# Attention with grouped heads, one core: V of the first group moved to SyncE's queue between two query loads, K of the second group asked for later

## The chip, the cores and the metric

The kernel runs on one core of a Trainium2 chip. The metric is the device time of one execution in microseconds (us). Engines are named as in the profile: PE is the matmul engine, PEld its weight loads, ACT is ScalarE, DVE VectorE, POOL GpSimd, SP SyncE. All times in a trace count from the start of its span; the span is 1.7 us shorter than the time (520.1 and 521.82 in the profiled execution).

## The reference

```python
B, Hq, Hkv, Sq, Sk, D = 16, 32, 8, 288, 512, 128        # bf16, values N(0,1) * 0.05
k = jnp.repeat(k, Hq // Hkv, axis=1)
v = jnp.repeat(v, Hq // Hkv, axis=1)
scores = jnp.einsum("bhqd,bhkd->bhqk", q, k) * D ** -0.5
p = softmax(scores, axis=-1)
return jnp.einsum("bhqk,bhkd->bhqd", p, v)
```

There are 16 x 8 = 128 groups of one K and V with 4 x 288 = 1152 query rows. A group is three blocks of work, so there are 384 blocks, counted from 0.

## The kernel before

Each block n is a set of score matmuls into PSUM (`op_s`, line L439), an exp on ACT from PSUM to SBUF (`op_exp`, L511 and L516), and, two blocks later, twelve matmuls with V (`op_pv`, L479). PSUM holds the scores of two blocks, so score block n needs exp n - 2 to be done. Queries and most K come transposed by DMA; K of groups 0 and 1 are loaded plainly and transposed on PE (`op_kt`, L404), with a copy out of PSUM on DVE (`op_kc`, L411). V is loaded, then copied by POOL into a layout with a column of ones (`op_vc`, L568).

The order at the start of each engine (cut; `...` marks cuts):

```python
first = [lambda i=i: op_q0(i) for i in range(2)]          # SyncE: queries of group 0, in two parts
first += [lambda: op_q(1), lambda: op_k(0, 2), lambda: op_v(0, None, 1, UG), lambda: op_q(2), lambda: op_q(3)]
...
@block.tensor
def _(eng):
    op_warm(WARM, BANK, ps_o[:, 1])                        # 5 matmuls of 512 columns on constants
    op_warm(1, P, ps_o[:, 1])
    op_kt(0, range(1), 0)                                  # transposes of the first K
    op_kt(0, range(1, NJ), 1)
    op_warm(1, P, ps_s[:, 1])
    for n in range(NS):
        op_s(n)
        ...
        if n == 1:
            op_kt(1, range(NJ), 1)                         # transposes of K of group 1
        if n >= LAG:
            op_pv(n - LAG)
...
@block.scalar
def _(eng):
    op_kd(eng, 0)                                          # K of group 0, 128 KB
    op_v(0, eng, 0, 1)                                     # V of group 0, 128 KB
    op_kd(eng, 1)                                          # K of group 1, 128 KB
    eng.activation(dum[:], nc.const_aps.tensor(0.0, [P, 1], FP32), ACTF.Exp)
    for n in range(NS):
        op_exp(n)
```

Of the kernel before, what the change touches and what calls it, by code (L numbers as in the profile page):

```python
# [7 lines left out]
ACTF = mybir.ActivationFunctionType  # L8
AX = mybir.AxisListType
BF16 = mybir.dt.bfloat16  # L10
FP32 = mybir.dt.float32
# [120 lines left out]
def bass_standalone__gqa_softmax__near_ridge_kernel(  # L132
# [5 lines left out]
):  # L138
    B, Hq, Sq, D = q.shape
    _, Hkv, Sk, _ = k.shape  # L140
    P = 128
    R = (Hq // Hkv) * Sq
# [45 lines left out]
    with ExitStack() as es:  # L188
# [66 lines left out]
        dum = main.enter_context(nc.sbuf_tensor("dum", [P, 1], FP32))  # L255
# [5 lines left out]
        def need(eng, waits):  # L261

            left = []
            for (s, n) in waits:
                key = (id(eng), s)
                if seen.get(key, 0) < n:
                    seen[key] = n
                    left.append((sem[s], n))
            return left

        def emit(eng, waits, fn):
            waits = need(eng, waits)
            for (s, n) in waits[:-1]:
                eng.wait_ge(s, n)
            ins = fn()
            if waits:
                ins.wait_op(waits[-1][0], waits[-1][1], "sem-ge")
            return ins
# [3 lines left out]
        def op_kd(eng, g):  # L282
            eng.dma_start(kd_sb[:, g], kd_v[:, g]).then_inc(sem["s_kd%d" % g], 16)

        def op_k(u, g0=0):
            eng = nc.sync
            sl = u % NSLOT
            if u >= NSLOT:
                for (s, n) in need(eng, [("s_s", NC * UG * (u - NSLOT + 1))]):
                    eng.wait_ge(s, n)  # L290
            eng.dma_start_transpose(
                kt_sb[:, sl, :, g0:UG].rearrange("d j g p -> d j (g p)"),
                k_v[(u * UG + g0) * P:(u + 1) * UG * P]
            ).then_inc(sem["us_k%d" % sl if u > 0 else "s_k2"], 16)

        def op_v(u, eng=None, g0=0, g1=UG):
            eng = eng or nc.sync
            sl = u % NSLOT
            if u >= NSLOT:
                for (s, n) in need(eng, [("s_vc", UG * (u - NSLOT + 1))]):  # L300
                    eng.wait_ge(s, n)
            eng.dma_start(
                vd_sb[:, sl, g0:g1], v_v[:, u * UG + g0:u * UG + g1]
            ).then_inc(sem["us_v%d" % sl if u > 0 else "s_v%d" % g0], 16)

        def op_q(g):
            eng = nc.sync
            if g >= NQ:
                for (s, n) in need(eng, [("s_s", NC * (g - NQ + 1))]):
                    eng.wait_ge(s, n)  # L310
            eng.dma_start_transpose(qt_sb[:, g % NQ], q_v[g * P:(g + 1) * P]).then_inc(sem["s_q%d" % (g % NQ)], 16)

        def op_q0(i):

            c0, c1 = ((0, TB), (TB, NT))[i]
            nc.sync.dma_start_transpose(qt_sb[:, 0, c0:c1], q_v[0:P, c0 * D:c1 * D]).then_inc(sem["s_qp%d" % i], 16)
# [82 lines left out]
        def op_kt(g, tiles, bank):  # L399

            eng = nc.tensor
            dst = ps_o[:, bank].bitcast(BF16)
            for x, j in enumerate(tiles):
                ins = emit(eng, [("s_id", 2), ("s_kd%d" % g, 16)], lambda: eng.transpose(  # L404
                    dst[:, x * P:(x + 1) * P], kd_sb[:, g, j * D:(j + 1) * D], ident[:]))
            ins.then_inc(sem["s_kp"], 1)
# [7 lines left out]
        def op_warm(n, w, dst):  # L414

            for x in range(n):
                nc.tensor.matmul(dst[:, 0:w], nc.const_aps.tensor(1.0, [P, P], BF16),
                                 nc.const_aps.tensor(1.0, [P, w], BF16), start=True, stop=True)

        def op_s(n):  # L420
            eng = nc.tensor
            g, i = n // NC, n % NC
            sl, gi = (g // UG) % NSLOT, g % UG
            waits = [have("k", g), have_q(g, i)]
            if n >= 2 + FIRST:
                waits.append(("s_e", n - 1))
            qg = qt_sb[:, g % NQ].rearrange("d t p -> d (t p)")
            todo = pieces(i)
            for x, (c, j, t, w) in enumerate(todo):
                if shared(n) and c + w == CH:  # L430
                    w -= W
                w_x = waits if x == 0 else []
                if n == 0 and x < 2:
                    w_x = [("s_k0", 1), waits[1]] if x == 0 else waits[:1]
                if n == 1 and x < 2:
                    w_x = [have_q(g, x)]
                if 2 <= n < 2 + FIRST:
                    w_x = w_x + [ready(n - 2, c // BANK)]
                ins = emit(eng, w_x, lambda: eng.matmul(  # L439
                    ps_s[:, n % 2, c:c + w], kt_sb[:, sl, j, gi, :], qg[:, t * P:t * P + w], start=True, stop=True))  # L440
                if n < FIRST and (c + w) % BANK == 0 and c + w < CH:
                    ins.then_inc(sem["s_s0"], 1)
            ins.then_inc(sem["s_s"], 1)

        def op_sy(n):

            eng = nc.tensor
            g = n // NC
            (t, j), = [(t, j) for t in range(NT) for j in range(NJ) if place(t, j) == (n % NC, CH - P)]
            emit(eng, [("s_ev", n - LAG - 1)], lambda: eng.matmul(  # L450
                ps_o[:, (n - LAG) % 2, BANK - W:BANK], kt_sb[:, (g // UG) % NSLOT, j, g % UG, :],
                qt_sb[:, g % NQ, t, P - W:P], start=True, stop=True))
# [9 lines left out]
        def op_pv(r):  # L462
            eng = nc.tensor
            g = r // NC
            sl, gi = (g // UG) % NSLOT, g % UG
            waits = [("s_vc", g + 1)]
            if 2 <= r < NS - 2:
                waits.append(("s_ev", r - 1))
            if r == NS - 2:
                waits.append(("s_e", NS - 1))  # L470


            todo = sequence(r % NC)
            for x, (t, j) in enumerate(todo):
                i, c = place(t, j)
                w_x = (waits if x == 0 else []) + [ready(g * NC + i, c // BANK)]
                if c == CH - P and shared(g * NC + i):
                    w_x.append(("s_yp", nth(g * NC + i)))
                ins = emit(eng, w_x, lambda: eng.matmul(  # L479
                    outs(r)[:, t - r % NC * TPC, :], pt(g, t, j), v_sb[:, sl, gi * NJ + j, 0:DV], start=(x == 0),  # L480
                    stop=(t not in [y[0] for y in todo[x + 1:]]), skip_group_check=True))
            ins.then_inc(sem["s_pv"], 1)
# [36 lines left out]
        def shared(n):  # L519
            return FIRST_SHARED <= n < NS - NC and (n - FIRST_SHARED) % EVERY == 0  # L520
# [102 lines left out]
                op0=ALU.is_lt, op1=ALU.add)).then_inc(sem["s_bad"], 1)  # L623


        first = [lambda i=i: op_q0(i) for i in range(2)]
        first += [lambda: op_q(1), lambda: op_k(0, 2), lambda: op_v(0, None, 1, UG), lambda: op_q(2), lambda: op_q(3)]

        sp = []
# [14 lines left out]
        @block.sync  # L644
        def _(eng):
            for fn in first:
                fn()
            for (_, fn) in sp:
                fn()
            choose(eng, "sp")  # L650

        @block.tensor
        def _(eng):
            op_warm(WARM, BANK, ps_o[:, 1])
            op_warm(1, P, ps_o[:, 1])
            op_kt(0, range(1), 0)
# [3 lines that stand above are left out]
                op_s(n)  # L660
                if shared(n):
                    op_sy(n)
                if n == 1:
                    op_kt(1, range(NJ), 1)
                if n >= LAG:
                    op_pv(n - LAG)
            op_pv(NS - 2)
            op_pv_last()
            emit(eng, [("s_ev", NS - 2), ("s_bad", 2)], lambda: eng.matmul(  # L669
                ps_o[0:1, NS % 2, 0:ALONE + 1], one_f[:], bad_sb[:, 1, :], start=True, stop=True)  # L670
            ).then_inc(sem["s_bad"], 1)
            choose(eng, "pe")

        @block.scalar
        def _(eng):
            op_kd(eng, 0)
            op_v(0, eng, 0, 1)
            op_kd(eng, 1)
            eng.activation(dum[:], nc.const_aps.tensor(0.0, [P, 1], FP32), ACTF.Exp)  # L679
            for n in range(NS):  # L680
                op_exp(n)
            op_ev_act()
            choose(eng, "act")
# [82 lines left out]
```

## Time and profile before

| | |
|---|---|
| time, median of the first 3 runs | 522.98 us (522.68 to 523.08) |
| time of the profiled execution | 521.82 us |
| span | 520.1 us |
| first exp starts | 5.27 us |
| PE waits for the last time before the end at | 9.71 us |
| last block's exp starts | 515.08 us |

The head of the page of this profile gives the span, each engine's busy time, and the share of TensorE's clock that the throttle granted, in forty slices:

```profile
span 520.1 us, 15350 instructions
...
PE 515.1 (99%) x6224; PEld 394.2 (76%) x6224; DVE 369.6 (71%) x1315; ACT 513.3 (99%) x393; POOL 79.4 (15%) x135
...
PEclk9999999999999999999999999999999999999999
```

PE and ACT are both full, and the clock row is at 9 throughout.

### The profile page before, as it was taken

The numbers are of one execution on the slowest core, as the hardware profiler recorded it, in microseconds if no ns is written. First come the engines' busy times: TensorE is split into PE (matmuls) and PEld (weight loads), VectorE is DVE, ScalarE is ACT, GpSimd is POOL, SyncE is SP. The second block draws the span as 40 slices with busy tenths as digits, with TensorE's granted clock in tenths as the row PEclk, the third lists the DMA queues.
The fourth block names the chain that finished last, engine by engine and source line by source line (L and its number), as shares of the span: only waits on it lengthen the run. The fifth ranks groups of instructions, "written<-read, shape, count | busy, mean of one in ns | idle before, by whom it ended". The sixth has DMA issues, their size and how long they took to land.

```text
span 520.1 us, 15350 instructions
## 1 busy us (share of the span) xinstructions
PE 515.1 (99%) x6224; PEld 394.2 (76%) x6224; DVE 369.6 (71%) x1315; ACT 513.3 (99%) x393; POOL 79.4 (15%) x135
## 2 busy tenths in 40 slices
PE   8999999999999999999999999999999999999997
PEld 4777777777777777777777777777777777777776
DVE  2767767777777677776776776767767767677776
ACT  7999999999999999999999999999999999999997
POOL 2111111111111111111111111111111111111110
PEclk9999999999999999999999999999999999999999
DMA  9999999999999998999999989999999999997212
GB/s 179 237 181 265 274 183 247 235 215 211 245 210 260 210 253 183 234 227 242 235 240 190 222 229 225 238 184 224 220 231 229 225 205 199 219 226 177 90 69 93
DMA packets 253110, 110.06 MB, mean 212 GB/s; under 512 B 219760, under 2 KB 236784, under 8 KB 253040
## 3 DMA queue, kind: packets, MB, share of 16 engines
q1 hardware_dynamic: 252608, 108.69, 98.2%
q8 instruction: 49, 0.80, 0.7%
q10 hardware_dynamic: 432, 0.39, 0.3%
q14 instruction: 21, 0.17, 0.1%
HBM read 17.04 MB, written 37.75 MB: 105 GB/s over the span
## 4 chain that ended last, share of the span: by engine, by line
ACT 98%; DMA 1%; issue 1%; DVE 0%; PE 0%
ACT pt_sb L516 97%; DMA qt_sb<-in_q_dram 1%; ACT pt_sb L511 1%; DVE o_sb L585 0%; DVE o_sb L595 0%; PE ps_s L479 0%; PE ps_s L439 0%; DVE rl_sb L575 0%; PE ps_o L669 0%; DVE bad_sb L621 0%; DVE flag_i L733 0%; DVE bad_sb L618 0%
## 5 line engine op out<-in xcount | busy, mean ns | idle before, releaser
L516 ACT ACTIVATE pt_sb<-ps_s 128x1536 bf16<-128x1536 f32 (+2 forms) x384 | 508.8, 1443 | 0.0
L479 PE MATMUL ps_o<-v_sb,pt_sb 128*128 128x129 bf16 x4584 | 322.5, 220 | 0.4 <-ACT pt_sb L516 0.4
L479 PEld LDWEIGHTS ps_o<-v_sb,pt_sb 128*128 128x128 bf16 x4584 | 282.7, 98 | 50.2 <-DVE o_sb L585 14.1
L439 PE MATMUL ps_s<-qt_sb,kt_sb 128*128 128x512 bf16 (+2 forms) x1536 | 309.3, 324 | 1.0 <-DMA qt_sb<-in_q_dram 1.0
L585 DVE TENSOR_TENSOR o_sb<-ps_o,rl_sb 128x384 bf16<-128x384 f32 x382 | 211.9, 555 | 9.3 <-DVE rl_sb L575 0.5
L439 PEld LDWEIGHTS ps_s<-qt_sb,kt_sb 128*128 128x128 bf16 x1536 | 123.5, 98 | 62.3 <-DMA qt_sb<-in_q_dram 1.7
L575 DVE RECIPROCAL rl_sb<-ps_o 128x3 f32<-128x3 f32 x382 | 68.2, 178 | 126.4 <-PE ps_o L479 125.0
L568 POOL COPY v_sb<-vd_sb 128x512 bf16<-128x512 bf16 x128 | 78.4, 613 | 429.7 <-PE ps_o L479 416.2
L549 DVE SCALAR_TENSOR_TENSOR u_sb<-u_sb,m_sb 128x120 f32<-128x120 f32 x126 | 35.6, 283 | 2.2
L556 DVE SCALAR_TENSOR_TENSOR pt_sb<-u_sb,e_sb 128x120 bf16<-128x120 f32 x63 | 17.8, 283 | 2.2
L549 DVE SCALAR_TENSOR_TENSOR u_sb<-m_sb 128x120 f32<-128x120 f32 x63 | 17.5, 277 | 0.0
L527 DVE TENSOR_SCALAR y_sb<-ps_o 128x120 f32<-128x120 f32 x63 | 15.9, 253 | 0.0
L540 DVE TENSOR_SCALAR m_sb<-t_sb 128x120 int32<-128x120 int32 x63 | 14.1, 223 | 2.2
L450 PE MATMUL ps_o<-qt_sb,kt_sb 128*128 128x120 bf16 x63 | 13.6, 217 | 0.0
L540 DVE TENSOR_SCALAR e_sb<-t_sb 128x120 int32<-128x120 int32 x63 | 13.6, 216 | 0.0
L533 DVE TENSOR_SCALAR t_sb<-y_sb 128x120 int32<-128x120 f32 x63 | 13.4, 213 | 0.0
L450 PEld LDWEIGHTS ps_o<-qt_sb,kt_sb 128*128 128x128 bf16 x63 | 6.2, 98 | 7.4
L411 DVE COPY kt_sb<-ps_o 128x128 bf16<-128x128 bf16 (+2 forms) x3 | 1.0, 336 | 5.4 <-PE ps_o L404 5.3
L511 ACT ACTIVATE pt_sb<-ps_s 128x512 bf16<-128x512 f32 x6 | 3.3, 617 | 1.5 <-PE ps_s L439 1.5
L679 ACT ACT_TABLE_LOAD x1 | 1.3, 1283 | 2.2 <-issue 2.2
L613 DVE TENSOR_REDUCE st_sb<-rl_sb 128x1 f32<-128x72 f32 (+1 forms) x16 | 3.5, 217 | 0.0
L611 DVE TENSOR_REDUCE st_sb<-rl_sb 128x1 f32<-128x72 f32 (+1 forms) x16 | 3.5, 216 | 0.0
(32 smaller groups left out, 13.1 us busy)
## 6 DMA issues: line engine op xcount, KB each, us to landing
out_dram<-o_sb SPq DMA_DIRECT2D x127, 288.0 KB, 3.8
vd_sb<-in_v_dram SPq DMA_DIRECT2D x31, 512.0 KB, 5.3
qt_sb<-in_q_dram SPq DMA_TRANSPOSE x129, 5.0
kt_sb<-in_k_dram SPq DMA_TRANSPOSE x32, 5.0
vd_sb<-in_v_dram SPq DMA_DIRECT2D x1, 384.0 KB, 4.3
out_dram<-o_sb SPq DMA_DIRECT2D x3, 96.0 KB, 1.6
kd_sb<-in_k_dram ACTq DMA_DIRECT2D x2, 128.0 KB, 2.9
vd_sb<-in_v_dram ACTq DMA_DIRECT2D x1, 128.0 KB, 3.2
```

Source lines behind the costliest of these rows:

```text
L439: ins = emit(eng, w_x, lambda: eng.matmul(ps_s[:, n % 2, c:c + w], kt_sb[:, sl, j, gi, :], qg[:, t * P:t * P + w], start=True, stop=True))
L450: emit(eng, [("s_ev", n - LAG - 1)], lambda: eng.matmul(ps_o[:, (n - LAG) % 2, BANK - W:BANK], kt_sb[:, (g // UG) % NSLOT, j, g % UG, :], ...
L479: ins = emit(eng, w_x, lambda: eng.matmul(outs(r)[:, t - r % NC * TPC, :], pt(g, t, j), v_sb[:, sl, gi * NJ + j, 0:DV], start=(x == 0), st ...
L516: emit(eng, waits, lambda: eng.activation(d, s, ACTF.Exp, scale=scale)).then_inc(sem["s_e"], 1)
L527: emit(eng, [("s_yb", nth(n) - NB), ("s_pv", n - LAG + 1)], lambda: eng.tensor_scalar(out=y_sb[:, b], in0=ps_o[:, (n - LAG) % 2, BANK - W: ...
L533: emit(eng, [("s_ym", 2 * (nth(n) - NB)), ("s_y", nth(n))], lambda: eng.tensor_scalar(out=t_sb[:, b], in0=y_sb[:, b], scalar1=Y_MUL, scala ...
L540: emit(eng, [("s_yp", nth(n) - NB), ("s_yb", nth(n))], lambda: eng.tensor_scalar(out=dst[:, b], in0=t_sb[:, b], scalar1=mask, scalar2=bits ...
L549: lambda: eng.scalar_tensor_tensor(out=u_sb[:, b, x], in0=src, scalar=QUARTIC[x], in1=m, op0=ALU.add, op1=ALU.mult)
L556: lambda: eng.scalar_tensor_tensor(out=pt_sb[:, n % NPT, CH - W:CH], in0=u_sb[:, b, 2], scalar=QUARTIC[3], in1=e_sb[:, b].bitcast(FP32), o ...
L568: emit(eng, waits, lambda: eng.tensor_copy(v_sb[:, sl, gi * NJ:(gi + 1) * NJ, 0:D], vd_sb[:, sl, gi].rearrange("p (j d) -> p j d", d=D))). ...
L575: emit(eng, [("s_pv", r + 1)], lambda: eng.reciprocal(rl_sb[:, TPC * r:TPC * (r + 1)].unsqueeze(2), outs(r)[:, :, D:DV])).then_inc(sem["s_ ...
L585: emit(eng, waits, lambda: eng.tensor_tensor(out=o_sb[:, g % NO, t0:t0 + TPC, :], in0=outs(r)[:, :, 0:D], in1=rl_sb[:, TPC * r:TPC * (r + ...
```

## The change

The intent: the very first query load shares the DMA engines with three loads from ACT's queue (from 3.6 to 3.8 us the trace has 70 packets of ACT's queue to 29 of SyncE's). If only the first K runs beside it, the first scores can start sooner. V of group 0 moves to SyncE's queue, behind the first part of the queries; K of group 1 is asked for once the first K has been transposed, and its transposes move behind score block 2.

```diff
-        first = [lambda i=i: op_q0(i) for i in range(2)]
+        first = [lambda: op_q0(0), lambda: op_v(0, None, 0, 1), lambda: op_q0(1)]
...
-                if n == 1:
+                if n == 2:
                     op_kt(1, range(NJ), 1)
...
             op_kd(eng, 0)
-            op_v(0, eng, 0, 1)
+            eng.activation(dum[:], nc.const_aps.tensor(0.0, [P, 1], FP32), ACTF.Exp)
+            for (s, n) in need(eng, [("s_k0", 2)]):
+                eng.wait_ge(s, n)
             op_kd(eng, 1)
-            eng.activation(dum[:], nc.const_aps.tensor(0.0, [P, 1], FP32), ACTF.Exp)
```

## The prediction

> **What bounds the kernel now.** I read the page's chain first, then asked the trace whether the engine it names really sets the pace, then went through the first 14 us, the only place the change touches.
>
> The chain that ended last names ScalarE (ACT) for nearly the whole span, with one DMA wait ahead of it:
>
> ```profile
> ACT 98%; DMA 1%; issue 1%; DVE 0%; PE 0%
> ```
>
> But section 1 of the page has PE as busy as ACT (both 99%), so I compared single exps with the score matmuls they read, in the timeline of a stretch in mid-kernel (start, duration, engine, line, operation):
>
> ```profile
> 262.76 0.82 PE L439 MATMUL ps_s<-qt_sb,kt_sb 128*128 128x512 bf16 x6
> 263.63 1.45 ACT L516 ACTIVATE pt_sb<-ps_s 128x1536 bf16<-128x1536 f32 x1
> 264.10 0.81 PE L439 MATMUL ps_s<-qt_sb,kt_sb 128*128 128x512 bf16 x3
> 264.96 1.45 ACT L516 ACTIVATE pt_sb<-ps_s 128x1536 bf16<-128x1536 f32 x1
> ```
>
> The scores end at 263.58 and 264.91 and the exps start 0.05 us later each: ACT waits for PE by a hair at every step, although the page books no idle time, because consecutive exps overlap. PE goes from one matmul to the next without a gap, one step per 1.33 us. So **PE is the bound** from some early point on, and any delay of PE after that point is final. The waits of PE give that point; there are only these:
>
> ```profile
> PE ps_o L669 <- DVE bad_sb L621: 1.0, 1, 1.0
> PE ps_s L439 <- DMA qt_sb<-in_q_dram: 1.0, 2, 0.8
> PE ps_o L417 <- PEq L751: 0.9, 1, 0.9
> PE ps_o L479 <- ACT pt_sb L516: 0.4, 1, 0.4
> ```
>
> The first is the final check, the third the start. The last one, in the timeline, is the turning point:
>
> ```profile
> 4.84 1.04 PE L439 MATMUL ps_s<-qt_sb,kt_sb 128*128 128x512 bf16 x4 [0.81 <-DMA qt_sb<-in_q_dram]
> 5.27 1.08 ACT L511 ACTIVATE pt_sb<-ps_s 128x512 bf16<-128x512 f32 x2 [1.52 <-PE ps_s L439]
> 8.09 0.81 PE L439 MATMUL ps_s<-qt_sb,kt_sb 128*128 128x512 bf16 x3
> 9.71 0.40 PE L479 MATMUL ps_o<-v_sb,pt_sb 128*128 128x129 bf16 x4 [0.36 <-ACT pt_sb L516]
> 10.85 1.17 POOL L568 COPY v_sb<-vd_sb 128x512 bf16<-128x512 bf16 x2 [5.77 <-DMA vd_sb<-in_v_dram]
> 11.93 0.84 PE L479 MATMUL ps_o<-v_sb,pt_sb 128*128 128x129 bf16 x12
> ```
>
> The first queries land at 4.79, PE starts the scores at 4.84, ACT starts exp 0 at 5.27 and runs exps 0, 1 and 2 without a gap. PE waits at 9.71 for exp 2, which ends at 9.65 (start 8.14 plus 1.51). From 9.71 PE never waits again until the final check. The end is thus 9.71 plus PE's work. What moves 9.71, or makes PE wait after it, moves the end one for one; nothing else does.
>
> [...] from 3.2 to 3.6 us both queues have packets, and then K of group 1 crowds out the transposes. [...] the first query load issues in 1.3 us and lands 4.0 us after its start. The activation-table load [...] is 1.28 us here and ends by 3.54, off the path in both kernels.
>
> **The change part by part.**
>
> (1) *ACT's queue loses V (128 KB) and has K of group 1 (128 KB) later.* Before, the packets of both run from 2.9 to 4.4 us, beside the first query load. Its own packets (512 of 256 bytes) run at about 0.1 us per 50 between 2.4 and 3.2 and end at 3.6 to 3.9, and it lands about 0.9 later. I estimate 3.4 for their end without that traffic, so a landing at about 4.3 instead of 4.79. Scores could start at 4.35 and exp 0 at 4.35 + 0.43 = 4.78.
>
> (2) *ACT now issues K of group 1 after the first transposed K is copied.* The two DVE copies end at 3.67 + 0.68 = 4.35. Issuing costs ACT's sequencer 0.38 to 0.51 us (its three issues before), in order ahead of exp 0. So exp 0 can't start before about 4.35 + 0.05 + 0.5 = 4.9. **Gain from (1) and (2) at exp 0: 5.27 - 4.9 = 0.35 us**, and 9.71 would become 9.36, if PE is ready.
>
> (3) *Transposes of K of group 1 go behind score block 2.* Issue at 4.4, landing 2.5 to 3.4 us later as the two K loads do now: about 7.2. Then 4 transposes (0.24 us until the next matmul) and the first PV (0.68), so score block 3 may start at about 8.15, against 8.09 now. It must start by about 9.36 - 1.1 = 8.26 to cost nothing (0.65 for the scores, 0.45 for 8 PV matmuls). Nearly hidden.
>
> (4) *SyncE's queue gets one more issue.* SyncE issues without a pause from 0.82 to 14 us, so its later loads all shift by one issue, 0.45 to 0.58: about 0.55. V's packets also come right after a transpose. There the ring drains badly, as the DMA view shows where the later V follows the transposed K (0.4 us stretches from 8.2 and from 8.8):
>
> ```profile
> q1 hardware_dynamic: 33, 0.02, 15.3%
> ...
> q1 hardware_dynamic: 124, 0.13, 89.6%
> ```
>
> V trickles until the transpose ahead of it has landed (8.91). So V of group 0 would flow from about 4.3 to 4.9 and the second query load behind it lands at about 6.5 instead of 6.04; it is needed by exp 1's second part at about 6.85. Hidden. V of group 0 itself lands by about 5.9, is copied in 0.61 and is needed at 7.4: hidden.
>
> What the 0.55 does further on:
> - Queries 1 (land at 7.82 now, 3.51 + 4.3) at about 8.4: score block 3 starts at 8.4, so the turning point is 8.4 + 1.1 = 9.5, not 9.36. **Gain left: 0.2 us.**
> - V of groups 1 to 3 (issue 6.53, lands at 10.8 now) at about 11.4; POOL copies group 1 in 0.61, so PV 3 can't start before 12.04. Before it was ready at 11.48 and PE took it at 11.93: slack 0.45. With a shift of 0.55 PV 3 is **0.1 us later than before**, whatever was gained in front of it.
> - Queries 2 (issue 7.16, land about 12.07) at 12.6, needed at 12.61: just met.
>
> The end follows the latest of these, not their sum: -0.35 (exp 0), -0.2 (queries 1), +0.1 (V of groups 1 to 3), 0 (queries 2). **Sum: +0.1 us**, 523.1. All instructions past the first few are the same ones in the same order (the comparison of the two programs shows only these moves), so nothing else changes over the other 505 us.
>
> **The rivals.**
> (a) *The head start holds*: if SyncE's issues shift by less than 0.45, or V of groups 1 to 3 lands no later because the DMA engines and not SyncE set its pace, the gain is 0.2 to 0.35: about 522.7. [...] Against it: the ring runs nearly dry at 8.2 to 8.8.
> (b) *The second query load is far later* (7 us or more[...]): exp 1 waits, 9.71 becomes 10, and the V behind it slips as well. 523.5 to 524. For it: the trickle of 0.6 to 0.9 us; against it: the packets behind can catch up, since 0.2 us hold up to 228 of them at the best rate.
> (c) *ACT's issue of K stretches*[...]; exp 0 starts at 5.3 or later. 523.0 to 523.6. Before, three ACT issues beside SyncE's first transpose took at most 0.51, so I give it little.
>
> **Range and chances.** All cases lie within a microsecond of 523, or 0.2%; the runs before spread over 0.4 us. I take 523.1, from 522.5 (rival a with the runs' spread) to 523.8 (rival b). A change of 2% would be 10 us, and no path of the first 14 us can give that: 0.99 for within 2%.
>
> **What would show it.** Right: exp 0 starts near 4.9; PE waits for q (not exp 2) before score block 3; a POOL copy of v_sb that starts near 11.4 with PE waiting for it before PV 3; from there steps of 1.33 us as before. Wrong: a second query load that lands after 6.9, exp 0 at 5.2 or later, PE waiting on the transposes of K of group 1, or a PE that waits nowhere after 9.4 (rival a). It would be wrong altogether if PE's pace of 1.33 us per step changed.

The sum came to +0.1 us, 523.1. That V holds up the query load behind it stands in it as my estimate; "the ring" is SyncE's DMA queue.

## The result, and the profile after

The changed kernel took **522.35 us** (median of 4 runs, 522.13 to 522.54); the kernel before took 523.03 in 4 runs (522.68 to 523.43). The ratio is 0.9987, with a 95% interval of 0.9969 to 1.0004. Ratios here are the mean time of one kernel's runs over that of the other's of the same rounds, so not quite the ratio of the medians. The interval takes in 1, so these runs alone don't show a gain. The verdict is "same" at 2%, as predicted, but 522.35 lies below the stated range (522.5 to 523.8): forecast was a loss of 0.1 us, found was a gain of 0.7 in the medians.

The page of the changed kernel, the same rows as above. It says something odd: this *faster* kernel has the *longer* span.

```profile
span 520.4 us, 15244 instructions
...
PE 510.5 (98%) x6118; PEld 394.6 (76%) x6224; DVE 369.5 (71%) x1315; ACT 513.6 (99%) x393; POOL 79.4 (15%) x135
...
PEclk9999999999999999999999999999999999999999
```

(The 106 matmuls fewer are missing records: the weight loads are 6224 in both.) The span of 520.4 belongs to a run of 522.13 us, near the median of its kernel; the span of 520.1 belongs to a run of 521.82, which is 1.16 us under the median of its own. **The trace I predicted from was of a faster execution than any of the timed ones beside it.**

First, the early timeline of the changed kernel (start, duration, engine, line, operation; in brackets the idle time before it and what ended it):

```profile
3.77 1.86 PE L439 MATMUL ps_s<-qt_sb,kt_sb 128*128 128x512 bf16 x4
...
4.11 0.34 ACTq L283 DMA_DIRECT2D kd_sb<-in_k_dram  x1
...
4.49 1.08 ACT L511 ACTIVATE pt_sb<-ps_s 128x512 bf16<-128x512 f32 x2 [1.77 <-PE ps_s L439]
...
5.90 1.29 PE L439 MATMUL ps_s<-qt_sb,kt_sb 128*128 128x512 bf16 x8 [0.26 <-DMA qt_sb<-in_q_dram]
...
8.20 0.82 PE L439 MATMUL ps_s<-qt_sb,kt_sb 128*128 128x512 bf16 x3
...
11.06 1.17 POOL L568 COPY v_sb<-vd_sb 128x512 bf16<-128x512 bf16 x2 [5.29 <-DMA vd_sb<-in_v_dram]
...
11.82 0.84 PE L479 MATMUL ps_o<-v_sb,pt_sb 128*128 128x129 bf16 x12
```

Scores start at 3.77 (4.84 before), exp 0 at 4.49 (5.27), score block 3 at 8.20 just after queries 1 landed at 8.15, and PV 3 as soon as POOL has copied V of group 1. The head start shrinks on the way: the exps of blocks 0 to 2 are 0.77 us earlier than in the first profile of before, those of blocks 3 to 5 0.41 earlier, and from block 7 to the last, 383, every exp is 0.15 or 0.16 us earlier. So 376 blocks add nothing: the middle is the same to 0.01 us.

Then the end. Here is the last block's first exp and the last two stores of before (ACT's and SyncE's rows of the timeline):

```profile
515.08 1.12 ACT L511 ACTIVATE pt_sb<-ps_s 128x512 bf16<-128x512 f32 x2
...
517.49 0.89 SPq L343 DMA_DIRECT2D out_dram<-o_sb  x2
```

and of the changed kernel:

```profile
514.93 1.12 ACT L511 ACTIVATE pt_sb<-ps_s 128x512 bf16<-128x512 f32 x2
...
517.34 1.19 SPq L343 DMA_DIRECT2D out_dram<-o_sb  x2
```

The two last stores take 0.89 us, from the start of the first issue to the end of the second, in one and 1.19 in the other. From the start of the last exp to the end of the span it takes 5.04 us before and 5.51 after. So the traces show a gain of 0.15 us at the start and a loss of 0.47 at the end, 0.3 us slower in all, while the timed runs say 0.7 us faster. Two questions: what makes the kernel before run 1.2 us slower at the median than in its profile, and what makes the end longer?

### The profile page after: what moved, and what is told of

Read it like the earlier page. It is cut to its first block, busy times and chain, and to the rows that moved or that the text cites. A ratio compares the mean times of both kernels' runs of the same rounds, so it can differ in the third digit from the quotient of the medians.

```text
span 520.4 us, 15244 instructions
## 1 busy us (share of the span) xinstructions
PE 510.5 (98%) x6118; PEld 394.6 (76%) x6224; DVE 369.5 (71%) x1315; ACT 513.6 (99%) x393; POOL 79.4 (15%) x135
## 4 chain that ended last, share of the span: by engine, by line
ACT 96%; PE 2%; issue 1%; DMA 1%; SPq 0%; DVE 0%
ACT pt_sb L516 96%; PE ps_s L439 1%; PE ps_o L479 1%; DMA qt_sb<-in_q_dram 1%; SPq L316 0%; ACT pt_sb L511 0%; DVE o_sb L585 0%; SPq L302 0%; DVE o_sb L595 0%; PE ps_s L479 0%; PE ps_o L404 0%; DVE rl_sb L575 0%; PE ps_o L669 0%; DVE bad_sb L621 0%; DVE flag_i L734 0%
## 5 line engine op out<-in xcount | busy, mean ns | idle before, releaser
L439 PE MATMUL ps_s<-qt_sb,kt_sb 128*128 128x512 bf16 (+2 forms) x1430 | 290.7, 320 | 4.8 <-DMA qt_sb<-in_q_dram 0.3
L417 PE MATMUL ps_o<-const-bfloat16-1.0 128*128 128x512 bf16 (+1 forms) x6 | 2.4, 573 | 0.9 <-PEq L752 0.9
```

The lines of the kernel that those rows point to most:

```text
L439: ins = emit(eng, w_x, lambda: eng.matmul(ps_s[:, n % 2, c:c + w], kt_sb[:, sl, j, gi, :], qg[:, t * P:t * P + w], start=True, stop=True))
```

## The experiments

All were checked for correct results and passed. They ran in four batches; the kernel before ran beside each.

### 1. Both kernels once more

The same two programs with a comment added.

> The kernel before, unchanged but for a comment: how far do two profiles and two sets of times of one kernel differ? Theory A (the early part of the program is the same in every run, and the spread of 0.5 us lies in the last store): exp 0 starts at 5.27 and the last exp (block 383) at 515.08 us within 0.03, while the span may differ from 520.1 by up to 0.5; the ratio to the kernel before is 1.000 within 0.001. Rival B (the whole program drifts from run to run): the last exp moves by 0.3 us or more from 515.08.

Measured: 522.82 us (522.60 to 522.89, 6 runs), ratio 1.000 (0.9988 to 1.0012). The new profile has a span of 521.1, 1.0 us longer than the first. Theory A falls; the last exp moved by as much as rival B asked, but not by its drift: exp 0 starts at 5.46, the last exp at 516.03, 0.95 us later than in the first profile, and *all* of that is there by block 2 and stays to within 0.05 us. The end (5.10 us) is as in the first profile. So one kernel has two kinds of beginning. Here is what PE did in the slow one:

```profile
4.81 2.74 PE L439 MATMUL ps_s<-qt_sb,kt_sb 128*128 128x512 bf16 x6 [0.89 <-DMA qt_sb<-in_q_dram]
...
7.77 1.31 PE L439 MATMUL ps_s<-qt_sb,kt_sb 128*128 128x512 bf16 x6
```

Six matmuls of 512 columns take 2.74 us; in the first profile (quoted in the prediction) four took 1.04. The weight loads of PE show the rate of one matmul after another:

```profile
5.21 0.15 PEld L439 LDWEIGHTS ps_s<-qt_sb,kt_sb 128*128 128x128 bf16 x1 [0.27 <-issue]
5.64 0.15 PEld L439 LDWEIGHTS ps_s<-qt_sb,kt_sb 128*128 128x128 bf16 x1 [0.28 <-issue]
6.07 0.15 PEld L439 LDWEIGHTS ps_s<-qt_sb,kt_sb 128*128 128x128 bf16 x1 [0.28 <-DMA qt_sb<-in_q_dram]
```

They are 0.43 us apart; in the steady part matmuls of 512 columns start 0.216 us apart. **PE ran at half rate** until 8.7 us, and ACT had to wait for it (0.62 us before exp 2), although the queries had landed at 4.76 and 5.97, no later than in the fast profile. The page's clock row shows 9 in every slice all the same, and the granted clock is 1.0.

That is because the views count the time ahead of the first clock record as full. The trace file has the record itself, though no view prints it (array `0/clock` of trace.npz): full clock is recorded from 8.77 us on in before_again, and from 3.86 in the first profile of before, where the warm-up matmuls of 512 columns ahead of it start 0.427 us apart and the first scores behind it 0.216. So it is the throttle after all, and the moment of its release is in every trace.

The kernel has warm-up matmuls (`op_warm`) from 0.86 us on. But in the kernel before PE then idles until the first queries land, 0.81 and 0.89 us in its two profiles. In the first profile full clock is recorded at 3.86, ahead of that idle time (4.02 to 4.84); in before_again the idle time (3.92 to 4.81) came first, and full clock at 8.77. That the idle time puts full clock off is a guess from these two profiles, which do not show it; experiment 3 tests it.

The changed kernel once more:

> The changed kernel, unchanged but for a comment. Theory A (a fixed gain of 0.15 us, as the two traces show from block 7 on; the 0.68 us between the medians is mostly the runs' spread): the last exp starts at 514.93 within 0.03, exp 0 at 4.49, and five rounds give a time 0.1 to 0.3 us (0.02 to 0.06%) under the kernel before. Rival B (the gain of 0.68 us is real and the profile does not show it): the ratio is again 0.9987, 0.6 us or more.

Measured: 522.35 us (522.10 to 522.58, 6 runs), ratio 0.9991 (0.9979 to 1.0004). Exp 0 at 4.50, but the last exp at 515.24, not 514.93: the copy of V of group 1 made PV 3 wait longer (that V landed at 11.32 instead of 11.01). The line that shows the wait:

```profile
12.13 0.84 PE L479 MATMUL ps_o<-v_sb,pt_sb 128*128 128x129 bf16 x12 [0.43 <-POOL v_sb L568]
```

So theory A's place of the last exp is missed, and the 0.7 us between the medians came again. Both profiles of this kernel run at full rate from about 6 us on (clock records at 5.99 and 5.18), and in neither has PE a gap before the first scores (busy for all of 3 to 4 us).

### 2. One part at a time

V moved, K of group 1 early (SyncE's list as after, ACT asks for both K at once, transposes as before):

```diff
+        first = [lambda: op_q0(0), lambda: op_v(0, None, 0, 1), lambda: op_q0(1)]
...
             op_kd(eng, 0)
-            op_v(0, eng, 0, 1)
             op_kd(eng, 1)
```

> One part alone: V of group 0 on SyncE's queue between the two first query loads; K of group 1 asked for at once on ScalarE's queue, its transposes where they were before. Theory A: the head start of exp 0 shrinks, because K of group 1 (128 KB) again runs beside the first query load: landing at about 4.2 instead of 3.57, exp 0 at about 4.65; SyncE's later loads stay late by one issue, so PV 3 still waits for V of groups 1 to 3 and the last exp starts at about 514.93, 0.15 under the kernel before, as in the whole change. Rival B (the late K brings the gain): exp 0 at 5.2 and the last exp no earlier than 515.08.

Measured: 523.13 us (522.12 to 523.78, 6 runs), ratio 1.0003 (0.9989 to 1.0017). Exp 0 was at 5.48 and the last exp at 516.31: rival B was nearer.

K late, its transposes behind score block 2 as in the change, V still second on ACT's queue:

```diff
-                if n == 1:
+                if n == 2:
                     op_kt(1, range(NJ), 1)
...
             op_kd(eng, 0)
             op_v(0, eng, 0, 1)
+            eng.activation(dum[:], nc.const_aps.tensor(0.0, [P, 1], FP32), ACTF.Exp)
+            for (s, n) in need(eng, [("s_k0", 2)]):
+                eng.wait_ge(s, n)
             op_kd(eng, 1)
-            eng.activation(dum[:], nc.const_aps.tensor(0.0, [P, 1], FP32), ACTF.Exp)
```

> The other part alone: K of group 1 asked for once the first K is transposed, its transposes behind score block 2; V of group 0 stays on ScalarE's queue as second load. Theory A: exp 0 starts at about 4.7 (V still runs beside the first query load), and SyncE's loads do not slip, so queries 1 land by 7.8 and V of groups 1 to 3 by 10.8 and neither costs anything: the last exp starts at about 514.6, 0.45 under the kernel before and 0.3 under the whole change. Rival B (the transposes of K of group 1, now waiting for their load, hold PE up): K lands after 7.3, PE waits for it, and the last exp is at 514.95 or later.

Measured: 522.72 us (521.85 to 523.37, 6 runs), ratio 0.9995 (0.9981 to 1.001). K of group 1 landed at 8.38, the last exp was at 516.55: as rival B said, and in these profiles (v_only and k_only) PE ran at half rate as well, its weight loads 0.43 us apart, to about 9.3 and 9.8 us (clock records at 9.32 and 9.78), after idle times of 1.05 and 0.95 us ahead of the first scores.

Neither part alone brings anything. The reason is in the landing of the first queries: 4.79 with V alone moved and 4.84 with K alone late, as in the kernel before, but 3.57 with both. What holds the first queries up in these runs is *a second load on ACT's queue right behind the first K*, whichever it is. Only the two parts together leave none. (It is not the only thing that moves them: in after_swap below, without such a load, they land at 4.21.) The DMA view of 2.4 to 3.0 us shows it. Before (per queue: packets, MB, share of the 16 engines; q1 is SyncE's queue, q10 ACT's):

```profile
q1 hardware_dynamic: 294, 0.08, 56.8%
q10 hardware_dynamic: 51, 0.04, 24.8%
```

and after:

```profile
q1 hardware_dynamic: 479, 0.12, 87.4%
q10 hardware_dynamic: 6, 0.00, 1.3%
```

### 3. Is it PE's rate?

If the rate is what counts, filling the wait of the kernel *before* with more warm-up matmuls must bring the gain without moving one load, and taking the warm-up out of the *changed* kernel must lose it. Before, filled:

```diff
-            op_warm(1, P, ps_s[:, 1])
+            op_warm(1 + 8, P, ps_s[:, 1])
```

> The kernel before with 8 more warm-up matmuls of 128 columns behind the transposes of the first K, so that PE is busy in the 0.8 to 0.95 us in which it waits for the first queries; no load is moved. Clock theory ([...] the change wins by taking that wait away): PE's 512-column matmuls are 0.216 us apart, not 0.427[...]; exp 2 starts by 8.4 (9.12 in the second profile of before), the last exp by 515.4, and the median is 521.9 to 522.4 us, 0.7 to 1.1 under the kernel before and no slower than the changed kernel. Load theory (the change wins by the earlier landing of the first queries): exp 0 stays at 5.3 to 5.5, and the median stays at 522.8 to 523.1.

Measured: **522.00 us** (521.80 to 522.13, 6 runs), ratio 0.9985 (0.9973 to 0.9997), the only interval here that leaves out 1. PE in its profile:

```profile
3.72 1.17 PE L417 MATMUL ps_s<-const-bfloat16-1.0 128*128 128x128 bf16 x9
4.84 1.15 PE L439 MATMUL ps_s<-qt_sb,kt_sb 128*128 128x512 bf16 x4
...
9.82 0.40 PE L479 MATMUL ps_o<-v_sb,pt_sb 128*128 128x129 bf16 x4 [0.21 <-ACT pt_sb L516]
```

The nine small matmuls keep PE busy, the scores start at 4.84 as ever and are at full rate from the second on, and the turning point is 9.82 (9.71 in the fast profile). Exp 2 starts at 8.26, the last exp at 515.19. The load theory falls: the queries still land at 4.79.

The two parts alone, with the wait filled in the same way (10 and 8 more matmuls):

> The V part alone, with 10 more warm-up matmuls in the wait for the first queries, so that the loads are judged at PE's full clock. Clock theory: exp 0 at about 5.3, exp 2 by 8.4, last exp at 515.1 to 515.5, that is no gain over the kernel before in its fast case (515.08), for the first queries land at 4.8 as before; median 522.0 to 522.4. Load theory: as v_only, median 523.1.

Measured: 522.50 us (522.33 to 522.75, 4 runs), ratio 0.9996 (0.998 to 1.0012); exp 2 at 8.31, last exp at 515.25. The start is as the clock theory said; the time is 0.1 over its range, which experiment 5 explains.

> The K part alone, with 8 more warm-up matmuls in the wait for the first queries. Clock theory: exp 0 at about 5.3; then, if K of group 1 lands at 8.4 again as in k_only, PE waits for it ahead of PV 0, score block 3 starts at about 9.3 and the last exp at about 515.8: the late K alone costs 0.7 us; if it lands by 7.4, the last exp is at 515.1. Load theory: as k_only, last exp at 516.5.

Measured: 522.05 us (521.86 to 522.16, 4 runs), ratio 0.9987 (0.9971 to 1.0003). K of group 1 landed at 7.67 this time, between the two cases named, and the last exp was at 515.14. So a K that lands at 7.67 costs nothing when PE runs at full rate; no run shows that for one that lands at 8.4.

The changed kernel without its first warm-up:

```diff
-            op_warm(WARM, BANK, ps_o[:, 1])
-            op_warm(1, P, ps_o[:, 1])
```

> The changed kernel without the warm-up matmuls ahead of the first K (PE's first work is the transposes at 3.05); loads, waits and order unchanged, and nothing on the way to the end waited for those matmuls. Clock theory: [...] score blocks 1 and 2 and PV 0 run at half rate, the last exp starts at 515.4 to 516.6 (514.93 and 515.24 in the two profiles of the changed kernel), and the median is 522.7 to 523.4. Load theory: first queries land at 3.6, exp 0 at 4.5, and the median stays at 522.3.

Measured: 523.03 us (522.40 to 523.25, 5 runs), ratio 1.0004 (0.999 to 1.0018). 0.68 us are lost at the median, and three of the five runs are above every run of the changed kernel, though the queries land at 3.53 and no instruction on the way to the end ever waited for those matmuls. In the profiled run, the fastest of the five (522.40), the full rate came at 6.9 us (clock record at 6.93):

```profile
3.70 1.87 PE L439 MATMUL ps_s<-qt_sb,kt_sb 128*128 128x512 bf16 x4
5.82 1.78 PE L439 MATMUL ps_s<-qt_sb,kt_sb 128*128 128x512 bf16 x8 [0.26 <-DMA qt_sb<-in_q_dram]
```

The second row took 1.29 us in the changed kernel. In this lucky run that cost nothing (last exp 514.86, earlier even than in my range), so that single profile does not bear out the theory; the five times do. I did not get a profile of a slow run of this kernel.

### 4. The queue after the first loads

In the changed kernel's profiles PV 3 waits for V of groups 1 to 3. Loading it ahead of the K of groups 2 and 3:

```diff
-        first += [lambda: op_q(1), lambda: op_k(0, 2), lambda: op_v(0, None, 1, UG), lambda: op_q(2), lambda: op_q(3)]
+        first += [lambda: op_q(1), lambda: op_v(0, None, 1, UG), lambda: op_k(0, 2), lambda: op_q(2), lambda: op_q(3)]
```

> The changed kernel with the load of V of groups 1 to 3 ahead of the transposed load of K of groups 2 and 3. In the two profiles of the changed kernel exp 6 lost 0.22 and 0.52 us because PV 3 waited for the copy of this V (it landed at 11.01 and 11.32). If that is the wait, V now lands by 10.2, no step is lost between exps 5 and 6, the last exp starts at about 514.7 (0.4 us under the first profile of before) and the median is 521.8 to 522.1, some 0.4 under the changed kernel. Rival (the queue's pace is what counts, and another load takes the place): queries 2 or K of group 2 land after 12.3, exp 6 is late all the same, and the median stays at 522.3.

Measured: 522.99 us (522.48 to 523.45, 6 runs), ratio 1.000 (0.9982 to 1.0017): the rival. V landed at 10.82, and the transposed loads behind it slipped: queries 2 landed at 13.42 (12.19 in the changed kernel) and exp 6 lost 1.0 us:

```profile
13.47 0.77 PE L439 MATMUL ps_s<-qt_sb,kt_sb 128*128 128x512 bf16 x3 [0.90 <-DMA qt_sb<-in_q_dram]
```

The same with V of group 0 behind both query loads of group 0:

> As after_v_first, and V of group 0 goes behind the second query load instead of between the two. The second query load then lands at about 5.0 instead of 5.85 [...], PE has no gap before 7 us, V of group 0 lands at about 6.2 and is copied by 6.9, before PV 0 needs it at 7.3. Queries 1 still land at about 8.1 and set score block 3. So the last exp starts as in after_v_first, 514.7, with less spread from run to run; median 521.8 to 522.1. Rival (V of group 0 is needed between the two loads): PV 0 waits for the copy past 7.4 and the last exp is at 514.9 or later.

Measured: 522.62 us (522.36 to 523.65, 6 runs), ratio 0.9999 (0.998 to 1.0017). The second query load landed at 5.06 and V of group 0 at 6.07, as expected, and exps 3 to 5 were 0.36 us ahead of the first profile of before; but queries 2 came at 12.75, block 6 lost 0.5 us, and the last exp was at 515.25. In both runs what one load gained on SyncE's queue, another paid.

### 5. The longer end

Over the profiles so far the end (last exp to end of span) falls into two groups: 5.00 to 5.10 us in before, before_again, before_fill, k_fill and k_only; 5.49 to 5.84 in the seven profiles with V of group 0 on SyncE's queue. Those seven have one SyncE instruction more (340 against 339 in the traces). In them a packet on the queue for instructions (q14) runs 0.6 to 0.9 us behind the start of the last store's issue; in the others it runs 1.3 to 1.4 behind. So is it the load, or the count of instructions? One needless wait (a semaphore long satisfied, in mid-kernel) added to the filled kernel before:

```diff
+        sp += [(NS / 2, lambda: nc.sync.wait_ge(sem["s_kd0"], 16))]
         sp.sort(key=lambda x: x[0])
```

> before_fill with one needless wait more in SyncE's instructions (a semaphore that is long satisfied, half-way through), so that SyncE has as many instructions as in the changed kernel. From the start of the last exp to the end of the span takes 5.0 to 5.1 us in every profile whose SyncE has the instruction count of the kernel before (before, before_again, before_fill, k_fill, k_only) and 5.5 to 5.85 where it has one more (after, after_again, v_only, v_fill, after_nowarm and the two variants)[...]. Fetch theory: this tail grows to about 5.5, the median from 522.0 to about 522.5. Rival (the tail is longer because V of group 0 goes through SyncE's queue): the tail stays at 5.05 and the median at 522.0.

Measured: 522.71 us (522.47 to 522.81, 6 runs), against 522.00 without the wait on another chip. The end takes 5.51 us. SyncE's row and, of 518.6 to 519.35, the instruction queue's:

```profile
517.73 1.18 SPq L343 DMA_DIRECT2D out_dram<-o_sb  x2
```

```profile
q14 instruction: 1, 0.01, 3.8%
```

The same two stores took 0.89 in before_fill, and no such packet fell in that stretch. So one more instruction, not the load, makes the end longer by 0.44 us (5.07 to 5.51), of the 0.7 between the two medians. What delays the last store is not shown: that it is a fetch of instructions (the "fetch theory") is a guess from that packet, which runs behind the start of that issue. Then twelve more SyncE instructions (24 such waits, which the trace shows as 12 instructions: 352 against 340) in the changed kernel, to move that packet away from the last stores:

> The changed kernel with 12 needless SyncE instructions (long satisfied waits, half-way through)[...]. Fetch theory: the time from the last exp to the end falls from 5.5 or more to about 5.05, and the median from 522.35 to 521.8 to 522.0: the change's whole gain at the start then shows, and this version is the fastest together with before_fill. Rival (V on SyncE's queue makes the tail long): 5.5 or more again, median 522.3.

Measured: **521.79 us** (521.41 to 522.07, 6 runs), ratio 0.9987 (0.9974 to 1.0001) on another chip, on which the kernel before had a median of 522.03 (521.73 to 523.62, 11 runs: more of its runs were fast ones). The end takes 4.99 us:

```profile
517.14 0.88 SPq L343 DMA_DIRECT2D out_dram<-o_sb  x2
```

Its instruction packet runs at 500.7. Its slowest run, 522.07, is below the fastest of the ten of the changed kernel, 522.10. This version has the lowest median of all, but its interval takes in 1 too. I did not run it and the changed kernel on one chip; 0.5 us between them is what the ends, 5.51 to 5.63 against 4.99, account for.

## Why the prediction was wrong

*What bounds the kernel* was right. From the turning point on, nothing moved: in the thirteen other profiles the distance to the first one of before, set by block 7 or 8, is the same to 0.02 us at block 383.

*Part 1, the landing of the first queries*: right in kind, too small. 3.57, not 4.3: the packets end at 3.1 (I had 3.4) and the landing follows 0.5 us later, not 0.9.

*Part 2, ACT's issue ahead of exp 0*: right, exp 0 follows the issue (4.11 + 0.34, then 4.49). With the first K earlier too, the head start was 0.77, not 0.35.

*Part 3*: K of group 1 landed at 7.06 (7.2) and cost nothing.

*Part 4, SyncE's loads slip by 0.55*: the issues did (0.54 for V of groups 1 to 3), the landings less. Queries 1 came at 8.15 and 8.17 (8.4), V of groups 1 to 3 at 11.01 and 11.32 (11.4), and PV 3 did wait for it, as named. The trickle behind a transpose is there: V of group 0, issued from 2.20, moved hardly a packet before the queries landed at 3.57 (its first one runs at 3.47). SyncE's queue from 3.0 to 3.6 us:

```profile
q1 hardware_dynamic: 39, 0.01, 24.4%
```

*The sum*: +0.1 us against the trace of before; measured -0.15 and +0.16 at the last exp in the two profiles. This sum held, though two of its terms were off (0.77 for 0.35 at exp 0, and V of groups 1 to 3 up to 0.4 early): the end follows the latest of them, as I had written, so the larger head start was lost again. **The step that failed is how I made a time of it**: "The end follows the latest of these ... Sum: +0.1 us, 523.1", with "All cases lie within a microsecond of 523". It adds a difference, read off a trace of an execution of 521.82 us, to a median of 522.98 of other executions. Had I compared these two numbers I should have seen that the trace and the median belong to different kinds of run, and asked for the cause. The kernel before, in 28 runs (4 beside the changed kernel and 24 beside the experiments), took 521.73 to 522.16 in 11 and 522.46 to 523.62 in 17. In the slow run that was profiled PE is still at half rate until 8.77 us, and the change takes that away, a gain of about 1 us (before_again 516.03 against 514.93 and 515.24 at the last exp), which no step of mine held. Only two profiles of before, one of each kind, tie its two groups of times to PE's rate; what ties the gain to it is that filling the wait alone brought 0.9 us at the medians, and taking out the warm-up cost 0.7.

*"Nothing else changes over the other 505 us"* failed too, by +0.47 us at the end. It hid part of the gain: about -1.0 in a slow start, +0.47 at the end, and -0.6 to -0.7 is what the medians show.

*The rivals*: (a) gave nearly the right time, 522.7, by luck, for its reason was another; (b) and (c) did not occur, the second query load landed at 5.85 and ACT's issue took 0.34. I had written that a change of "PE's pace" would make the prediction wrong altogether, but looked for it at 1.33 us per step in the steady part, not in the first 9 us.

## What to carry to other kernels

Before adding a predicted difference to a median, check that the profiled execution took the median's time; if not, explain that gap first. Where a kernel begins with warm-up matmuls, look for idle time behind them: here filling a wait of 0.8 to 0.9 us with eight idle matmuls brought 0.9 us at the median, more than moving any load gained. When a program grows by an instruction, look at both ends of the trace: here one SyncE instruction more made the end 0.44 us longer.
